# First 512 tokens loaded as four transposes of 512 by 256 and contracted in depth pairs, with the weight loads moved to another queue

## Chip, cores and metric

One core of one Trainium2 chip. The metric is device microseconds of one execution. All comparisons are between runs of the fast state, each with runs of the kernel before on the same chip. A ratio is the mean time of one kernel's fast runs over the mean of the other's in the same rounds, so it is not quite the ratio of the medians quoted beside it.

## The reference

Two attention blocks share one input x (2048 tokens, width 1024, bf16), and a gate mixes them.

```python
x = A_x
g = _sigmoid((x * gate_w).sum(-1, keepdims=True))
a = _A_ref(x, A_wqkv, A_wo)      # linear attention: qkv, phi, state, output projection
b = _B_ref(x, B_wqkv, B_wo)      # dilated local attention: qkv, 8 keys a query, output projection
return g * a + (1 - g) * b
```

What matters here is the first product of the kernel: v of block B, that is x @ B_wqkv[:, 2048:3072], 16 tiles of 128 tokens by two halves of 512 columns, each eight matmuls deep: 256 matmuls. It needs x transposed, depth on the partitions.

## The kernel before

The kernel records operations, and a list scheduler puts them in an order for each engine. `after` and the tiles that an operation reads and writes become waits on semaphores; `prio` orders operations that are ready.

```python
def load_x(t, prio):           # one tile of 128 tokens, all 1024 of depth: 256 KB, transposed by the DMA
    e_, r = t // 8, t % 8
    return P.op("sp", lambda e: e.dma_start_transpose(xT[:, :, t * 128:(t + 1) * 128], x2[e_, r * 128:(r + 1) * 128, :]), ...)

def load_w(slot, half, src, c0, prio, d0=0, d1=8, eng="sp", after=()):   # depth blocks d0 to d1: 128 KB each
    ...
load_x(0, 0)
load_w(0, 0, Bw, 2048, 0.1, 0, 2, "act")      # first weight half, four pieces: two from ScalarE
load_w(0, 0, Bw, 2048, 0.2, 2, 4, "act")
load_w(0, 0, Bw, 2048, 0.3, 4, 6)             # and two from Sync
load_w(0, 0, Bw, 2048, 0.4, 6, 8)
for t in range(1, NT):
    load_x(t, 3 + t)
for d in range(0, 8, 2):
    load_w(0, 1, Bw, 2560, 6.1 + 0.1 * d, d, d + 2)   # second weight half, Sync
# ... (cut)
for i in range(WARM):          # 9 matmuls on zeros, to raise the clock
    ...
for t, half in [(4 * b + i, half) for b in range(NT // 4) for half in range(2) for i in range(4)]:
    bank = main.next()
    step = 2 if t == 0 else 8
    for d in range(0, 8, step):
        o = group(bank, xs, w, [xr, ws[0].part((d, d + step), (half * 512, half * 512 + 512))], d, d + step)
    move(vt[:, :], bank.ap, 512, bank, vt.all())     # evict to SBUF, then store to HBM
```

In the profile, line 1313 is the matmul inside `group`, 1292 the DMA inside `load_w`, 1287 the transposing DMA of `load_x`.

Of the kernel before, what the change touches and what calls it, by code (L numbers as in the profile page):

```python
# [13 lines left out]
D = 1024  # L14
# [1088 lines left out]
def build_kernel(nc, A_x, A_wqkv, A_wo, B_x, B_wqkv, B_wo, gate_w, out):  # L1103
    del B_x
    S = A_x.shape[1]
    NT = S // 128
    HS = S // 2
    x2 = A_x[0].rearrange("(m e) d -> e m d", e=2)
# [5 lines left out]
    def SB(shape, dtype, name, at=None):  # L1114
        n = SZ[dtype]
        for d in shape[1:]:
            n *= d
        if at is None:
            at = base[0]
            base[0] += (n + 31) // 32 * 32  # L1120
        uid[0] += 1
        h = nc.alloc_sbuf_tensor_at("%s_%d" % (name, uid[0]), list(shape), dtype, offset=at)
        return Tile("S", h, at, list(shape), dtype)
# [34 lines left out]
    def hb(p0, p1, half):  # L1158
        return [("H%d" % half, p0, p1, None)]

    xT = SB([128, 8, S], BF16, "xT")
    qT = SB([128, 8, S], BF16, "qT")
    kT = SB([128, 8, S], BF16, "kT")
    ws = [SB([128, 8, 1024], BF16, "w%d" % i) for i in range(4)]
# [7 lines left out]
    gwb = SB([128, 1024], BF16, "gwb")  # L1172
# [30 lines left out]
    xn = Ring([SB([128, 1024], BF16, "xn%d" % i, at=az.t[i].lo) for i in range(2)])  # L1203
# [14 lines left out]
    act = lambda n: 0.19 + n / 1200.0  # L1218
    dps = lambda n: 0.14 + n / 960.0

    def plan(seen):

        P = Prog(nc, nc.alloc_semaphore)
# [58 lines left out]
        Bw = B_wqkv.rearrange("(dc p) f -> p dc f", p=128)  # L1282
        Bo = B_wo.rearrange("(dc p) f -> p dc f", p=128)

        def load_x(t, prio):
            e_, r = t // 8, t % 8
            return P.op("sp", lambda e: e.dma_start_transpose(xT[:, :, t * 128:(t + 1) * 128], x2[e_, r * 128:(r + 1) * 128, :]),  # L1287
                        1.5, writes=[xT.part((0, 8), (t * 128, (t + 1) * 128))], prio=prio, chan="x%d" % t, lat=1.3)

        def load_w(slot, half, src, c0, prio, d0=0, d1=8, eng="sp", after=()):  # L1290
            n = d1 - d0
            return P.op(eng, lambda e: e.dma_start(ws[slot][:, d0:d1, half * 512:half * 512 + 512], src[:, d0:d1, c0:c0 + 512]), 0.4 + 0.2 * n,  # L1292
                        writes=[ws[slot].part((d0, d1), (half * 512, half * 512 + 512))], prio=prio, chan="w%d_%d_%d" % (slot, half, d0), lat=0.55 * n, after=after)

        load_x(0, 0)
        load_w(0, 0, Bw, 2048, 0.1, 0, 2, "act")
        load_w(0, 0, Bw, 2048, 0.2, 2, 4, "act")
        load_w(0, 0, Bw, 2048, 0.3, 4, 6)
        load_w(0, 0, Bw, 2048, 0.4, 6, 8)
        for t in range(1, NT):  # L1300
            load_x(t, 3 + t)
        for d in range(0, 8, 2):
            load_w(0, 1, Bw, 2560, 6.1 + 0.1 * d, d, d + 2)
        P.op("sp", lambda e: e.dma_start(gwb[:, :], gate_w[None, :].to_broadcast([128, D])), 0.6, writes=[gwb.all()], prio=29, chan="gw", lat=0.8)


        main = Pool(banks[0:7])

        def group(bank, lhs, rhs, reads, lo=0, hi=8):
            def fn(e):  # L1310
                last = None
                for dc in range(lo, hi):
                    last = e.matmul(bank.ap(), lhs(dc), rhs(dc), start=(dc == 0), stop=(dc == 7))  # L1313
                return last
            return P.op("pe", fn, (hi - lo) * mm(512), reads=reads, writes=[bank.iv])
# [13 lines left out]
        def x_tile(t):  # L1329
            return (lambda dc: xT[:, dc, t * 128:(t + 1) * 128]), xT.part((0, 8), (t * 128, (t + 1) * 128))  # L1330

        def x_chunk(u):
            return (lambda dc: xT[:, dc, u * 512:(u + 1) * 512]), xT.part((0, 8), (u * 512, (u + 1) * 512))

        def w_half(slot, half):
            return (lambda dc: ws[slot][:, dc, half * 512:half * 512 + 512]), ws[slot].part((0, 8), (half * 512, half * 512 + 512))

        def w_cols(slot, j):
            return (lambda dc: ws[slot][:, dc, j * 128:(j + 1) * 128]), ws[slot].part((0, 8), (j * 128, (j + 1) * 128))
# [11 lines left out]
        for i in range(WARM):  # L1351
            P.op("pe", lambda e: e.matmul(banks[7].ap(), warm[:, 0:128], warm[:, :], start=True, stop=True), 0.43, reads=[warm.all()], writes=[banks[7].iv], prio=-1)


        early = {(2, 0): (1, 0, Bw, 1024, 21), (4, 1): (2, 0, Bw, 0, 22), (7, 1): (1, 1, Bw, 1536, 23), (10, 1): (2, 1, Bw, 512, 24),
                 (12, 1): (3, 0, Aw, 1024, 25), (14, 1): (3, 1, Aw, 1536, 26)}
        for t, half in [(4 * b + i, half) for b in range(NT // 4) for half in range(2) for i in range(4)]:
            vt, vs = vst.next()
            xs, xr = x_tile(t)
            bank = main.next()  # L1360
            w, wr = w_half(0, half)
            step = 2 if t == 0 else 8
            for d in range(0, 8, step):
                o = group(bank, xs, w, [xr, ws[0].part((d, d + step), (half * 512, half * 512 + 512))], d, d + step)
            move(vt[:, :], bank.ap, 512, bank, vt.all())
            P.op("sp", lambda e, t=t, vt=vt, half=half: e.dma_start(vB_hbm[t * 128:(t + 1) * 128, half * 512:half * 512 + 512], vt[:, :]), 0.6, reads=[vt.all()],
                 writes=[hb(t * 128, (t + 1) * 128, half)], chan="vst%d" % vs, lat=0.5, prio=5)
            if (t, half) in early:
                load_w(*early[t, half], after=[o])
        load_w(0, 0, Aw, 2048, 30)  # L1370
        load_w(0, 1, Aw, 2560, 31)


        for t in range(NT):
            xt, xs_ = xn.next()
            P.op("sp", lambda e, t=t, xt=xt: e.dma_start(xt[:, :], x2[t // 8, (t % 8) * 128:(t % 8) * 128 + 128, :]), 0.6, writes=[xt.all()], chan="xn%d" % xs_, lat=1.0)
            P.op("dve", lambda e, t=t, xt=xt: e.scalar_tensor_tensor(out=xt[:, :], in0=xt[:, :], scalar=1.0, in1=gwb[:, :], op0=ALU.mult, op1=ALU.mult,
                                                                      accum_out=gt[:, t:t + 1]), dps(1024), reads=[xt.all(), gwb.all()], writes=[xt.all(), gt.part((t, t + 1))],
                 prio=1000 + len(P.ops) + 80)
# [7 lines left out]
        main = Pool(banks[0:4])  # L1387
# [80 lines left out]
        for e_ in range(2):  # L1468
            if True:
                for j in range(8):  # L1470
                    for isq in range(2):
                        for u in (2 * e_, 2 * e_ + 1):
                            bank = main.next()
                            w, wr = w_cols(1 + isq, j)
                            xs, xr = x_chunk(u)
# [10 lines left out]
        for c in range(4):  # L1486
            for I in range(2):
                P.op("sp", lambda e, c=c, I=I: e.dma_start(ws[1][32 * c:32 * c + 32, 4 * I:4 * I + 4, :],
                                                           A_wo[512 * I + 128 * c:512 * I + 128 * c + 128, :].rearrange("(r e) f -> e r f", e=32)), 0.6,
                     writes=[ws[1].part((4 * I, 4 * I + 4), (0, 1024))], prio=40, chan="wo%d_%d" % (c, I), lat=0.9)  # L1490
# [25 lines left out]
        for t in range(NT):  # L1516
            pkt, _ = pk.next()
            azt, _ = az.next()
            xs, xr = x_tile(t)
            for r in range(4):  # L1520
                bank = main.next()
                w, wr = w_half((3, 0)[r // 2], r % 2)
# [16 lines left out]
        main = Pool(banks)  # L1539
# [158 lines left out]
    for _ in range(PASSES):  # L1698
        got = plan(seen)
        seen = got[2]  # L1700
        if best is None or got[0].span < best[0].span:
            best = got
    P, flag_op = best[:2]
# [52 lines left out]
```

## Time and profile before

| | before |
|---|---|
| median of 6 runs | 495.50 us (495.07 to 496.56) |
| span of the profiled run | 493.6 us |
| first real matmul | 5.62 us |
| second tile of x landed | 7.97 us |
| second weight half landed | 14.70 us |
| first matmul of the k projection (end of the first product) | 61.80 us |
| from there to the end | 431.83 us |

The last three rows matter most. The first product is 256 matmuls, 0.2158 us from start to start when nothing holds them: 55.24 us. From 5.62 to 61.80 it took 56.18, so 0.94 us were lost there. The landing times come from the records of the DMA semaphores in the trace; the lines of the profile are shown in the prediction.

### The profile page before, as it was taken

To read this page: it belongs to the slowest core of one execution; us is meant where nothing else is said; L and a number is where in the kernel's file an instruction comes from. 1 tells how busy PE (TensorE), PEld (TensorE's weight loads), DVE (VectorE), ACT (ScalarE), POOL (GpSimd) and SP (SyncE) were. 2 spreads that over 40 slices of the span, in tenths; PEclk is the share of its full clock that TensorE was granted. 3 is DMA by queue.
4 is the path that set the end of the run, shared out by engine and by line. 5 is a ranking of instruction groups with operands and counts; after the bars stand their busy time and mean duration, and the time that the engine had idled before them with its cause. 6 is when DMAs were issued, how large, how long until landed. Compare 5 with 4: busy or idle time off the path is not lost.

```text
span 493.6 us, 11394 instructions
## 1 busy us (share of the span) xinstructions
PE 477.7 (97%) x5055; PEld 226.2 (46%) x5121; DVE 274.7 (56%) x487; ACT 166.9 (34%) x287; POOL 5.1 (1%) x27
## 2 busy tenths in 40 slices
PE   8999999999999999999999999999999999999995
PEld 3444444444444445545554544444444444444442
DVE  2112345899676785564555555596865735524443
ACT  2111111222334345656565465455432223020000
POOL 3000000000000000000000000000000000000000
PEclk9999999999999999999999999999999999999999
DMA  8989992222003155111010100503564325101122
GB/s 225 212 206 322 307 371 62 86 86 85 14 23 110 29 161 141 28 36 35 24 35 25 35 3 3 171 1 80 124 182 117 76 38 153 65 1 66 65 85 68
DMA packets 51067, 48.80 MB, mean 99 GB/s; under 512 B 20161, under 2 KB 38977, under 8 KB 51010
## 3 DMA queue, kind: packets, MB, share of 16 engines
q1 hardware_dynamic: 50466, 47.47, 34.5%
q8 instruction: 42, 0.69, 0.6%
q10 hardware_dynamic: 544, 0.52, 0.3%
q14 instruction: 15, 0.12, 0.1%
HBM read 34.34 MB, written 9.44 MB: 89 GB/s over the span
## 4 chain that ended last, share of the span: by engine, by line
PE 89%; DMA 3%; SPq 3%; issue 2%; DVE 2%; ACT 1%; ACTq 0%
PE ps_all L1313 71%; PE ps_all L1634 11%; PE ps_all L1405 2%; PE ps_all L1424 2%; DMA rb<-rc_hbm 1%; SPq L1287 1%; PE ps_all L1506 1%; SPq L1598 1%; DMA w<-in_B_wqkv_dram 1%; PE ps_all L1431 1%; DMA rc_hbm<-ra 1%; DVE zsel L1548 1%; SPq L1292 1%; DVE pq L1326 0%; PE ps_all L1585 0%
## 5 line engine op out<-in xcount | busy, mean ns | idle before, releaser
L1313 PE MATMUL ps_all<-w,xT 128*128 128x512 bf16 x921 | 207.5, 380 | 5.4 <-issue 4.3
L1313 PE MATMUL ps_all<-xT,w 128*128 128x512 bf16 x748 | 167.5, 379 | 2.3 <-issue 1.7
L1313 PEld LDWEIGHTS ps_all<-w,xT 128*128 128x128 bf16 x960 | 91.3, 98 | 109.8 <-DMA xT<-in_A_x_dram 1.8
L1313 PEld LDWEIGHTS ps_all<-xT,w 128*128 128x128 bf16 x768 | 73.7, 98 | 89.1 <-issue 1.8
L1634 PE MATMUL ps_all<-w,qT 128*128 128x512 bf16 (+1 forms) x259 | 55.3, 373 | 0.3
L1634 PEld LDWEIGHTS ps_all<-w,qT 128*128 128x128 bf16 x264 | 25.8, 98 | 29.7
L1324 DVE TENSOR_SCALAR e<-e 128x512 bf16<-128x512 bf16 x64 | 18.3, 291 | 33.8 <-ACT e L1320 17.2
L1344 DVE CAST vst<-ps_all 128x512 bf16<-128x512 f32 x15 | 10.4, 692 | 44.0 <-PE ps_all L1313 44.0
L1411 ACT ACTIVATE E<-ps_all 128x1824 bf16<-128x1824 f32 (+1 forms) x18 | 30.4, 1687 | 9.8 <-PE ps_all L1405 9.0
L1322 ACT ACTIVATE e<-ps_all 128x512 bf16<-128x512 f32 x32 | 19.1, 597 | 42.8 <-PE ps_all L1313 42.8
L1414 DVE TENSOR_TENSOR E<-E,msk 128x1824 bf16<-128x1824 bf16 (+1 forms) x18 | 19.8, 1102 | 22.1 <-ACT E L1411 22.1
L1638 DVE SCALAR_TENSOR_TENSOR o<-ps_all,gm,xT 128x512 bf16<-128x512 f32 (+1 forms) x25 | 18.2, 730 | 23.0 <-PE ps_all L1634 22.8
L1320 ACT ACTIVATE e<-ps_all 128x512 bf16<-128x512 f32 x32 | 19.1, 597 | 26.8 <-PE ps_all L1313 25.8
L1345 ACT ACTIVATE vst<-ps_all 128x512 bf16<-128x512 f32 x17 | 10.1, 597 | 47.7 <-PE ps_all L1313 47.7
L1274 DVE TENSOR_TENSOR mx<-mx,kT 128x1024 bf16<-128x1024 bf16 x32 | 20.8, 688 | 9.3 <-ACT kT L1345 9.2
L1274 DVE TENSOR_TENSOR mx<-mx,qT 128x1024 bf16<-128x1024 bf16 x32 | 20.8, 687 | 6.9 <-ACT qT L1348 6.7
L1443 DVE TENSOR_TENSOR qT<-ps_all,L 128x456 bf16<-128x456 f32 (+1 forms) x36 | 21.0, 627 | 6.2 <-ACT L L1441 5.0
L1326 DVE SCALAR_TENSOR_TENSOR pk<-ps_all,e 128x512 bf16<-128x512 f32 x32 | 21.9, 688 | 0.7
L1440 ACT ACTIVATE L<-ps_all 128x456 f32<-128x456 f32 (+1 forms) x36 | 17.8, 547 | 12.4 <-PE ps_all L1424 12.4
L1345 ACT ACTIVATE kT<-ps_all 128x512 bf16<-128x512 f32 x16 | 9.6, 597 | 35.8 <-PE ps_all L1313 35.8
L1601 DVE TENSOR_TENSOR xT<-xT,rb 128x512 bf16<-128x512 bf16 x24 | 16.3, 689 | 8.7 <-DMA rb<-rc_hbm 8.5
L1348 ACT ACTIVATE qT<-ps_all 128x512 bf16<-128x512 f32 x16 | 9.6, 597 | 31.5 <-PE ps_all L1313 31.5
(72 smaller groups left out, 284.1 us busy)
## 6 DMA issues: line engine op xcount, KB each, us to landing
rb<-rc_hbm SPq DMA_DIRECT2D x32, 256.0 KB, 5.1
w<-in_A_wqkv_dram SPq DMA_DIRECT2D x6, 1024.0 KB, 8.5
v<-vB_hbm SPq DMA_DIRECT2D x36, 128.0 KB, 2.9
vB_hbm<-vst SPq DMA_DIRECT2D x32, 128.0 KB, 5.9
w<-in_B_wqkv_dram SPq DMA_DIRECT2D x4, 1024.0 KB, 9.0
xn<-in_A_x_dram SPq DMA_DIRECT2D x16, 256.0 KB, 2.7
out_dram<-o SPq DMA_DIRECT2D x15, 256.0 KB, 2.0
w<-in_A_wo_dram SPq DMA_DIRECT2D x8, 256.0 KB, 4.1
```

Of the source, the lines that this page charges most:

```text
L1274: P.op("dve", lambda e, m=m, op=op: e.tensor_tensor(m[:, 0:n], m[:, 0:n], src, op), 0.08 + n / 1920.0, reads=[m.all(), reg], writes=[m.all()],
L1313: last = e.matmul(bank.ap(), lhs(dc), rhs(dc), start=(dc == 0), stop=(dc == 7))
L1320: P.op("act", lambda e: e.activation(e_[:, :], bank.ap(), ACT.Exp), act(512), reads=[bank.iv], writes=[e_.all()])
L1322: P.op("act", lambda e: e.activation(e_[:, :], bank.ap(), ACT.Exp, accum_out=qe[:, col:col + 1]), act(512) + 0.1, reads=[bank.iv], writes= ...
L1324: P.op("dve", lambda e: e.tensor_scalar(e_[:, :], e_[:, :], 1.0, 1e-6, op0=ALU.min, op1=ALU.add), 0.25, reads=[e_.all()], writes=[e_.all()])
L1326: P.op("dve", lambda e: e.scalar_tensor_tensor(out=dst, in0=bank.ap(), scalar=0.0, in1=e_[:, :], op0=ALU.max, op1=ALU.add), dps(512), read ...
L1345: fa = lambda e: e.activation(dst, src(), ACT.Copy)
L1411: P.op("act", lambda e: e.activation(E[:, 0:32 * nq].rearrange("p (j q) -> p j q", j=4), ps[:, 4:8, 0:8 * nq], ACT.Exp), act(32 * nq), rea ...
L1414: P.op("dve", lambda e: e.tensor_tensor(ev(), ev(), m[:, :, :].rearrange("p r q -> p (r q)")[:, None, :].to_broadcast([128, 16, 2 * nq]), ...
L1443: P.op("dve", lambda e, L=L, h=h, q0=q0: e.tensor_tensor(qT[:, :, q0:q0 + nq], SO[h].ap(0, n).rearrange("p (c q) -> p c q", c=8), L[:, 0:n ...
L1634: last = e.matmul(bank.ap(0, f1 - f0), qT[:, dc, t * 128:(t + 1) * 128], ws[3][:, dc, f0:f1], start=(dc == 0), stop=(dc == 7))
L1638: P.op("dve", lambda e, bank=bank, o_=o_, t=t, n=n, i0=i0, i1=i1, tgt=tgt, c0=c0: e.scalar_tensor_tensor(out=o_[:, i0 * 128:i1 * 128].rear ...
```

## The change

Its intent is to have the start consume the loads as they come: four transposing loads of 512 tokens by 256 of depth, so that after the first of them four banks can each take two matmuls; a block of eight tiles, so that the second weight half is wanted later; and later loads held back so that they don't compete. All four first weight pieces and the second weight half now come from ScalarE's queue. Cut to its core:

```diff
-        load_x(0, 0)
-        load_w(0, 0, Bw, 2048, 0.1, 0, 2, "act")
-        load_w(0, 0, Bw, 2048, 0.2, 2, 4, "act")
-        load_w(0, 0, Bw, 2048, 0.3, 4, 6)
-        load_w(0, 0, Bw, 2048, 0.4, 6, 8)
-        for t in range(1, NT):
-            load_x(t, 3 + t)
         for d in range(0, 8, 2):
-            load_w(0, 1, Bw, 2560, 6.1 + 0.1 * d, d, d + 2)
+            load_w(0, 0, Bw, 2048, 0.1 + 0.1 * d, d, d + 2, "act")
+            P.op("sp", lambda e, d=d: e.dma_start_transpose(xT[:, d:d + 2, 0:512], x2[0, 0:512, 128 * d:128 * d + 256]), ...)
+        for t in range(4, 8):
+            load_x(t, 4 + t)
 ...
-        for t, half in [(4 * b + i, half) for b in range(NT // 4) for half in range(2) for i in range(4)]:
+        for t, half in [(t, half) for t0, n in ((0, 8), (8, 4), (12, 4)) for half in range(2) for t in range(t0, t0 + n)]:
+            if t < 4 and half == 0:
+                if t == 0:
+                    first = [main.next() for _ in range(4)]
+                    for d in range(0, 8, 2):
+                        for t_ in range(4):
+                            if d == 6 and t_ == 0:
+                                o_w = o
+                            o = group(first[t_], x_tile(t_)[0], w, [...], d, d + 2)
+                    for d in range(0, 8, 4):
+                        load_w(0, 1, Bw, 2560, 3 + 0.1 * d, d, d + 4, "act", after=[o_w])
+                bank = first[t]
 ...
+                if (t, half) == (5, 0):
+                    for t_ in range(8, NT):
+                        load_x(t_, 4 + t_, [o])
```

(Cut: assumed DMA durations of the scheduler; the loads of gate_w and of plain x, which also wait for tile 5; and the load of the next weight slot, now tied to the second half of tile 1 and not to the first of tile 2.) In the changed kernel `group` is line 1309 and the new transposes are line 1297.

More of the change, by code (lines that the diff above doesn't have):

```diff
@@ L1283, in plan, with load_x @@
         Bo = B_wo.rearrange("(dc p) f -> p dc f", p=128)
-        def load_x(t, prio):
+        def load_x(t, prio, after=()):
             e_, r = t // 8, t % 8
             return P.op("sp", lambda e: e.dma_start_transpose(xT[:, :, t * 128:(t + 1) * 128], x2[e_, r * 128:(r + 1) * 128, :]),
-                        1.5, writes=[xT.part((0, 8), (t * 128, (t + 1) * 128))], prio=prio, chan="x%d" % t, lat=1.3)
+                        1.5, writes=[xT.part((0, 8), (t * 128, (t + 1) * 128))], prio=prio, chan="x%d" % t, lat=1.15, after=after)
         def load_w(slot, half, src, c0, prio, d0=0, d1=8, eng="sp", after=()):
@@ L1292, in load_w @@
             return P.op(eng, lambda e: e.dma_start(ws[slot][:, d0:d1, half * 512:half * 512 + 512], src[:, d0:d1, c0:c0 + 512]), 0.4 + 0.2 * n,
-                        writes=[ws[slot].part((d0, d1), (half * 512, half * 512 + 512))], prio=prio, chan="w%d_%d_%d" % (slot, half, d0), lat=0.55 * n, after=after)
-        load_x(0, 0)
-        load_w(0, 0, Bw, 2048, 0.1, 0, 2, "act")
-        load_w(0, 0, Bw, 2048, 0.2, 2, 4, "act")
-        load_w(0, 0, Bw, 2048, 0.3, 4, 6)
-        load_w(0, 0, Bw, 2048, 0.4, 6, 8)
-        for t in range(1, NT):
-            load_x(t, 3 + t)
-        for d in range(0, 8, 2):
-            load_w(0, 1, Bw, 2560, 6.1 + 0.1 * d, d, d + 2)
-        P.op("sp", lambda e: e.dma_start(gwb[:, :], gate_w[None, :].to_broadcast([128, D])), 0.6, writes=[gwb.all()], prio=29, chan="gw", lat=0.8)
+                        writes=[ws[slot].part((d0, d1), (half * 512, half * 512 + 512))], prio=prio, chan="w%d_%d_%d" % (slot, half, d0), lat=0.42 * n, after=after)
+        for d in range(0, 8, 2):
+            load_w(0, 0, Bw, 2048, 0.1 + 0.1 * d, d, d + 2, "act")
+            P.op("sp", lambda e, d=d: e.dma_start_transpose(xT[:, d:d + 2, 0:512], x2[0, 0:512, 128 * d:128 * d + 256]),
+                 1.3, writes=[xT.part((d, d + 2), (0, 512))], prio=d / 2, chan="xd%d" % d, lat=1.2)
+        for t in range(4, 8):
+            load_x(t, 4 + t)
         main = Pool(banks[0:7])
@@ L1352, in plan @@
             P.op("pe", lambda e: e.matmul(banks[7].ap(), warm[:, 0:128], warm[:, :], start=True, stop=True), 0.43, reads=[warm.all()], writes=[banks[7].iv], prio=-1)
-        early = {(2, 0): (1, 0, Bw, 1024, 21), (4, 1): (2, 0, Bw, 0, 22), (7, 1): (1, 1, Bw, 1536, 23), (10, 1): (2, 1, Bw, 512, 24),
+        early = {(1, 1): (1, 0, Bw, 1024, 21), (4, 1): (2, 0, Bw, 0, 22), (7, 1): (1, 1, Bw, 1536, 23), (10, 1): (2, 1, Bw, 512, 24),
                  (12, 1): (3, 0, Aw, 1024, 25), (14, 1): (3, 1, Aw, 1536, 26)}
-        for t, half in [(4 * b + i, half) for b in range(NT // 4) for half in range(2) for i in range(4)]:
+        for t, half in [(t, half) for t0, n in ((0, 8), (8, 4), (12, 4)) for half in range(2) for t in range(t0, t0 + n)]:
             vt, vs = vst.next()
             xs, xr = x_tile(t)
-            bank = main.next()
             w, wr = w_half(0, half)
-            step = 2 if t == 0 else 8
-            for d in range(0, 8, step):
-                o = group(bank, xs, w, [xr, ws[0].part((d, d + step), (half * 512, half * 512 + 512))], d, d + step)
+            if t < 4 and half == 0:
[5 more added lines that the diff above has]
+                                o_w = o
+                            o = group(first[t_], x_tile(t_)[0], w, [xT.part((d, d + 2), (t_ * 128, t_ * 128 + 128)), ws[0].part((d, d + 2), (0, 512))], d, d + 2)
+                    for d in range(0, 8, 4):
+                        load_w(0, 1, Bw, 2560, 3 + 0.1 * d, d, d + 4, "act", after=[o_w])
+                bank = first[t]
+            else:
+                bank = main.next()
+                o = group(bank, xs, w, [xr, ws[0].part((0, 8), (half * 512, half * 512 + 512))])
+                if (t, half) == (5, 0):
+                    x_op = o
+                    for t_ in range(8, NT):
+                        load_x(t_, 4 + t_, [o])
             move(vt[:, :], bank.ap, 512, bank, vt.all())
@@ L1369, in plan @@
                 load_w(*early[t, half], after=[o])
+        P.op("sp", lambda e: e.dma_start(gwb[:, :], gate_w[None, :].to_broadcast([128, D])), 0.6, writes=[gwb.all()], prio=29, chan="gw", lat=0.8, after=[x_op])
         load_w(0, 0, Aw, 2048, 30)
@@ L1375, in plan @@
             xt, xs_ = xn.next()
-            P.op("sp", lambda e, t=t, xt=xt: e.dma_start(xt[:, :], x2[t // 8, (t % 8) * 128:(t % 8) * 128 + 128, :]), 0.6, writes=[xt.all()], chan="xn%d" % xs_, lat=1.0)
+            P.op("sp", lambda e, t=t, xt=xt: e.dma_start(xt[:, :], x2[t // 8, (t % 8) * 128:(t % 8) * 128 + 128, :]), 0.6, writes=[xt.all()], chan="xn%d" % xs_, lat=1.0, after=[x_op])
             P.op("dve", lambda e, t=t, xt=xt: e.scalar_tensor_tensor(out=xt[:, :], in0=xt[:, :], scalar=1.0, in1=gwb[:, :], op0=ALU.mult, op1=ALU.mult,
```

## The prediction

> **What bounds the kernel now.** I read the page first: the shares of busy time, then the chain that ended last.
>
> ```profile
> PE 477.7 (97%) x5055; PEld 226.2 (46%) x5121; DVE 274.7 (56%) x487; ACT 166.9 (34%) x287; POOL 5.1 (1%) x27
> ...
> PE 89%; DMA 3%; SPq 3%; issue 2%; DVE 2%; ACT 1%; ACTq 0%
> ```
>
> TensorE is busy 97% of a 493.6 us span and carries 89% of the chain. A change to the loads can win only time in which TensorE waits or runs slowly, and this change touches only the start. So next I read the chain in order of time for the first 60 us.
>
> ```profile
> 4.64 2.18 SPq L1287
> ...
> 9.36 0.47 SPq L1292
> ...
> 9.87 4.83 DMA w<-in_B_wqkv_dram
> 14.70 0.05 issue
> 14.74 0.61 PE ps_all L1313 x2
> 15.35 0.05 issue
> 15.40 10.74 PE ps_all L1313 x49
> ```
>
> Up to 14.7 us the chain runs through load issues on the Sync queue and then a weight load; after that it is matmuls in unbroken pieces. This looks like 14 us of load-bound start, but it is not: a chain says what released the last wait, not how long the wait was. So I read how the weight loads of TensorE stand in time from 5 to 18 us.
>
> ```profile
> 5.62 0.13 PEld L1313 LDWEIGHTS ps_all<-w,xT 128*128 128x128 bf16 x2 [1.26 <-DMA xT<-in_A_x_dram]
> 6.02 0.15 PEld L1313 LDWEIGHTS ps_all<-w,xT 128*128 128x128 bf16 x1 [0.28 <-issue]
> 6.45 0.15 PEld L1313 LDWEIGHTS ps_all<-w,xT 128*128 128x128 bf16 x1 [0.28 <-issue]
> 6.76 0.75 PEld L1313 LDWEIGHTS ps_all<-w,xT 128*128 128x128 bf16 x4 [0.15 <-issue]
> 8.02 5.72 PEld L1313 LDWEIGHTS ps_all<-w,xT 128*128 128x128 bf16 x28 [0.51 <-DMA xT<-in_A_x_dram]
> 14.00 0.17 PEld L1313 LDWEIGHTS ps_all<-w,xT 128*128 128x128 bf16 x2 [0.26 <-DMA w<-in_B_wqkv_dram]
> 14.74 3.35 PEld L1313 LDWEIGHTS ps_all<-w,xT 128*128 128x128 bf16 x17 [0.56 <-DMA w<-in_B_wqkv_dram]
> ```
>
> The real work starts at 5.62 us. Two waits follow, for the second x tile (until 8.02) and for the second weight half (until 14.74). The bracketed gaps overstate them, because weight loads run ahead of the matmuls. I therefore measured start to start of the matmul records. Steady spacing is 0.216 us (28 of them from 8.02 run at that). Above it stand: 5.621 to 6.753 us, three intervals of which two are at about 0.43, an excess of 0.48 us; 7.618 to 8.019, an excess of 0.185; 14.288 to 14.741, an excess of 0.237. Sum 0.90 us. The first evictions of the banks check this:
>
> ```profile
> 8.04 0.60 ACT L1345 ACTIVATE vst<-ps_all 128x512 bf16<-128x512 f32 x1 [4.99 <-PE ps_all L1313]
> ...
> 9.96 0.60 ACT L1345 ACTIVATE vst<-ps_all 128x512 bf16<-128x512 f32 x1 [1.32 <-PE ps_all L1313]
> ...
> 11.68 0.69 DVE L1344 CAST vst<-ps_all 128x512 bf16<-128x512 f32 x1 [5.78 <-PE ps_all L1313]
> ...
> 13.41 0.60 ACT L1345 ACTIVATE vst<-ps_all 128x512 bf16<-128x512 f32 x1 [2.86 <-PE ps_all L1313]
> ...
> 15.38 0.60 ACT L1345 ACTIVATE vst<-ps_all 128x512 bf16<-128x512 f32 x1 [1.38 <-PE ps_all L1313]
> ```
>
> A group of eight matmuls takes 1.73 us when nothing holds it (11.68 to 13.41). Group two came 1.92 after group one and group five 1.97 after group four: excesses of 0.19 and 0.24, the same two waits. So the whole start holds 0.90 us to be won behind the first matmul, 0.18% of the span, and of these 0.48 are not a wait.
>
> **What the Trainium skill says.** First, "TensorE: Matmul & The Clock Gate", section "What's actually happening": the array runs at half clock until it has been busy for about one free-running window of 3413 ns. The trace agrees: warm-up matmuls from 1.25 us at 0.427 spacing, full clock recorded from 6.62 us. That is the 0.48 us: the first three intervals of real work straddle the switch. Second, the same page, "Wait — 56ns, not 53.3ns?", gives 215.7 ns start to start for 512 warm columns; the trace has 216. Third, "DMA: Bandwidth & Descriptors", section "Issuing engines are not separate DMA queues": loads issued from ScalarE and Sync share the same 16 engines, so moving a load to another issuer saves issue time alone. The trace agrees: while the second weight piece (ScalarE) and the first transpose (Sync) were both in flight, each half microsecond moved about 110 packets of 1 KB and 144 of 256 B, against some 560 small ones for a transpose alone. Fourth, same page, "Latency and other measured facts": a transposing load was measured there at 261 GB/s. This trace has 1024 packets of 256 B, 18 ns each on 16 engines: 1.15 us for 256 KB, or 228 GB/s; I use that.
>
> **The change, part by part.**
>
> *Start of the first matmul.* Before, it needs tile 0 transposed (256 KB) and the first weight piece (256 KB). After, it needs the first transpose of 512 by 256 (256 KB) and the same weight piece. Before, these land at 5.58 and 3.53 us. In the new one the transpose is again the first on Sync at 0.8 us, beside the same two first ScalarE loads. If it also makes 1024 packets of 256 B, as its size suggests, it lands at about 5.6. No gain and no loss: 0.0 us. This is my least certain term, since no transposing load of this shape is in the trace.
>
> *Clock.* Warm-up and start stay, so about 0.48 us of half speed stays: 0.0.
>
> *Second wait.* Before, matmul 9 needs tile 1, landed at 7.97; by then the engines had moved four weight pieces and two transposes. After, matmul 9 needs the second transpose; the four weight pieces now come all from ScalarE beside it, so when it lands the engines have moved at most the same six transfers. Four pieces at 256 x 48 ns / 16 = 0.77 us and two transposes at 1.15 are 5.4 us of engine time in both kernels. So it lands at 7.9 to 8.1 and the 0.185 us wait mostly stays; if the transposes get more of the engines, up to 0.18 is won. I take -0.05.
>
> *Later depth pairs.* Third and fourth transpose land at about 9.1 and 10.3 (1.15 apart); needed at 8.02 + 1.73 = 9.75 and 11.5. No wait. The pieces are eight matmuls long, against two in before, so each covers its successor's load.
>
> *Second weight half.* Before, it is 1 MB in four pieces behind three tiles, wanted after 32 matmuls: the 0.237 us wait. After, a block of eight tiles puts it behind 64 matmuls, at about 5.6 + 64 x 0.216 + 0.7 = 20.1 us. It is issued when the third depth pair is done, about 11.5, and its engine time is 3.1 us. This wait goes: -0.24.
>
> *Tiles 4 to 7.* They follow at 1.15 us on the queue, so the fourth ends near 14.9 if alone; needed at 13.4, 15.1, 16.8, 18.5. The second weight half is in flight with tiles 6 and 7. Two transposes and 1 MB of weights are 5.4 us of engine time from about 12.1, ending near 17.5 plus 0.4 of landing: 18.0 against the 18.5 at which tile 7 is wanted. It fits, by half a microsecond. 0.0.
>
> *Everything later.* The order of TensorE's matmul groups after the first stage is the same in both builds; the differences on VectorE and ScalarE are swapped copies up to the first attention block, where both have slack (56% and 34% busy). Later x tiles, now held until tile 5 is done, are wanted from 34 us on and issued from 17: no cost.
>
> Sum: -0.05 - 0.24 = -0.3 us. From the measured 495.43 that is **495.1 us**.
>
> **The rivals.**
>
> (1) The start is load-bound and the change removes all of it. For: the chain shows loads up to 14.7 us, and the wanted bytes per matmul fall, since each weight piece now serves four tiles. Against: TensorE was at its steady spacing for all but 0.42 us of waiting. At most 0.42 plus some of the clock's 0.48: 494.5 to 495.0.
>
> (2) The new shape lands later: short rows of 512 B, or four weight pieces ahead of the first transpose on the shared engines. For: the 30% share that a transpose got beside weights. Against: the second piece was as much beside it before. If it lands 1 us later, TensorE also idles longer before its clock rises: 496 to 497.
>
> (3) The freed waits return as one for tile 6 or 7 beside the second weight half (margin 0.5 us by my sum): 495.3 to 496.
>
> (4) The clock switches elsewhere in its free-running window: half a microsecond either way, in either kernel; with the before runs spread from 495.07 to 496.56 this alone hides the gain.
>
> **Range and chances.** Centre 495.1. Half a microsecond of spread for clock and runs, half for the landing of the new transpose, added as independent about 0.7; for 8 in 10 that is 494.2 to 496.1. Two per cent is 9.9 us, over ten times what the start holds; only a failure of the new loads could be that slow. Faster 0.005, same 0.985, slower 0.01.
>
> **What would show it.** In the new profile: first real matmul at 5.4 to 5.9 us with a wait for xT; a remaining wait for xT before the ninth matmul of at most 0.3; no wait for w near matmul 65; no wait for tiles 4 to 7; steady 1.73 us per group from about 8 us on; first k projection about 0.3 us earlier than 61.80. I would be wrong if the first transpose lands after 6.5, if full clock comes later than 7.5, or if a wait appears at tiles 6 or 7.

## The result, and the profile after

The changed kernel took 499.90 us (median of 6 runs, 498.04 to 501.45) against 495.50 (6 runs, 495.07 to 496.56): ratio 1.0086, 95% interval 1.006 to 1.0112. It is slower by 4.4 us, less than 2% but clear of the noise, and outside the predicted range.

From the page of the changed kernel, the shares of busy time and the chain that ended last:

```profile
PE 480.8 (96%) x5055; PEld 227.4 (46%) x5121; DVE 276.7 (55%) x489; ACT 165.8 (33%) x285; POOL 5.1 (1%) x27
...
PE 88%; DMA 4%; SPq 3%; DVE 2%; issue 2%; ACT 0%; ACTq 0%
```

Nothing stands out: one per cent less TensorE, one more DMA. The chain in order of time (start, length, what) of the changed kernel says where:

```profile
13.21 9.29 DMA xT<-in_A_x_dram
22.50 0.14 issue
22.63 9.19 PE ps_all L1309 x34
```

One transposing load, issued at 13.21 us, ended a wait at 22.50: more than nine microseconds, where the kernel before shows 3.8 as the median of its sixteen. It is tile 7. The weight loads of TensorE in the changed kernel (columns: start, length, engine and line, count, idle time before and what ended it):

```profile
6.22 0.14 PEld L1309 LDWEIGHTS ps_all<-w,xT 128*128 128x128 bf16 x2 [1.85 <-issue]
6.63 0.15 PEld L1309 LDWEIGHTS ps_all<-w,xT 128*128 128x128 bf16 x1 [0.27 <-issue]
...
10.35 9.60 PEld L1309 LDWEIGHTS ps_all<-w,xT 128*128 128x128 bf16 x45 [0.16 <-issue]
22.60 1.51 PEld L1309 LDWEIGHTS ps_all<-w,xT 128*128 128x128 bf16 x8 [2.65 <-issue]
24.38 0.15 PEld L1309 LDWEIGHTS ps_all<-w,xT 128*128 128x128 bf16 x1 [0.27 <-issue]
...
27.34 2.69 PEld L1309 LDWEIGHTS ps_all<-w,xT 128*128 128x128 bf16 x13 [0.24 <-issue]
```

Read the lines with x1: a load by itself every 0.43 us is a matmul at half clock. The start shows that until 10.35 us (in before until 6.75), and after the pause before 22.60 it comes again, until 27.34. The clock records agree: full from 10.23, half from 23.88 to 27.29.

The balance of this run against before: first matmul 0.63 us later (6.25 against 5.62); half clock 3.6 us against 0.5; the wait for tile 7, 2.35 us, against two small ones of 0.4 together. The k projection starts at 67.48 against 61.80, 5.68 later, and from there to the end it is 431.66 against 431.83. So the loss is in the first product, all of it.

What the DMA engines did shows in the stretches (columns: stretch, its length, busy time of the five engines, clock, mean DMA share, GB/s). Before:

```profile
5.00:7.00 2.00, 1.65 (x6) 0.56 (x6) 0.43 (x2) 0.00 (x0) 0.61 (x3) 1.00 1.15 308
7.00:9.00 2.00, 1.98 (x10) 0.77 (x9) 0.00 (x0) 0.60 (x1) 0.00 (x0) 1.00 1.12 250
...
15.00:20.00 5.00, 4.95 (x24) 2.29 (x24) 0.69 (x1) 1.19 (x2) 0.00 (x0) 1.00 0.87 208
```

And the changed kernel:

```profile
5.00:7.00 2.00, 1.02 (x3) 0.28 (x3) 0.43 (x2) 0.00 (x0) 0.63 (x3) 1.00 1.17 211
7.00:9.00 2.00, 2.00 (x6) 0.73 (x5) 0.00 (x0) 0.00 (x0) 0.00 (x0) 1.00 1.31 204
...
15.00:20.00 5.00, 4.95 (x24) 2.25 (x23) 1.59 (x3) 1.19 (x2) 0.00 (x0) 1.00 1.18 146
```

The last two columns are to be read together. The engines are busier (1.18 against 0.87 from 15 to 20 us) and move less (146 GB/s against 208). The records of the single packets say how: a 1 KB piece of weights took 46 to 48 ns when its kind was alone; from 15.5 to 17 us of the changed kernel the mean was 210 to 350 ns, and 50 to 97 ns for the 256 B pieces of the transposes, which take 18 alone. In both stretches (5 to 9 and 15 to 20 us) transposes from Sync and plain weight loads from ScalarE are in flight together. The second profile of the same kernel (changed_again, below) is milder in the later one: 50 to 108 ns for weights from 15.5 to 21 us, and 202 GB/s.

**Theory A**: transposing and plain loads on two queues at once share the 16 engines badly. The engines lose throughput, and the loads that are wanted later (third and fourth weight piece, second weight half) take the time of those wanted now (second transpose, tile 7). **Rivals**: the new shape of 512 by 256 is slow in itself; there are simply too many bytes; the size of the pieces; the idle gap ahead of the first matmul and the clock it costs.

### The profile page after: what moved, and what is told of

Read it like the earlier page. It is cut to its first block, busy times and chain, and to the rows that moved or that the text cites. A ratio compares the mean times of both kernels' runs of the same rounds, so it can differ in the third digit from the quotient of the medians.

```text
span 499.1 us, 11394 instructions
## 1 busy us (share of the span) xinstructions
PE 480.8 (96%) x5055; PEld 227.4 (46%) x5121; DVE 276.7 (55%) x489; ACT 165.8 (33%) x285; POOL 5.1 (1%) x27
## 4 chain that ended last, share of the span: by engine, by line
PE 88%; DMA 4%; SPq 3%; DVE 2%; issue 2%; ACT 0%; ACTq 0%
PE ps_all L1309 70%; PE ps_all L1645 11%; PE ps_all L1416 2%; PE ps_all L1435 2%; DMA xT<-in_A_x_dram 2%; SPq L1297 2%; DMA rb<-rc_hbm 1%; PE ps_all L1517 1%; SPq L1609 1%; SPq L1287 1%; DMA rc_hbm<-ra 1%; PE ps_all L1442 1%; DVE zsel L1559 1%; DVE pq L1322 0%; PE ps_all L1596 0%
## 5 line engine op out<-in xcount | busy, mean ns | idle before, releaser
L1309 PE MATMUL ps_all<-w,xT 128*128 128x512 bf16 x921 | 210.4, 384 | 8.1 <-issue 4.3
L1340 DVE CAST vst<-ps_all 128x512 bf16<-128x512 f32 x17 | 11.6, 691 | 48.5 <-PE ps_all L1309 48.5
L1422 ACT ACTIVATE E<-ps_all 128x1824 bf16<-128x1824 f32 (+1 forms) x18 | 30.4, 1688 | 10.2 <-PE ps_all L1416 9.5
L1341 ACT ACTIVATE vst<-ps_all 128x512 bf16<-128x512 f32 x15 | 9.0, 597 | 53.3 <-PE ps_all L1309 53.3
```

Source lines behind the costliest of these rows:

```text
L1309: last = e.matmul(bank.ap(), lhs(dc), rhs(dc), start=(dc == 0), stop=(dc == 7))
L1341: fa = lambda e: e.activation(dst, src(), ACT.Copy)
L1422: P.op("act", lambda e: e.activation(E[:, 0:32 * nq].rearrange("p (j q) -> p j q", j=4), ps[:, 4:8, 0:8 * nq], ACT.Exp), act(32 * nq), rea ...
```

## The experiments

Landing times (us) from the profiled run of each kernel; for the kernel before and its variant the second column is tile 1. "Lost" is the start of the k projection minus the first matmul minus 55.24; "waits" are the pauses in it, less one spacing each, and "half clock" what the matmul intervals in half-clock time exceed 0.216 us by. Each row is one profile, so a difference of some tenths between rows is not a finding.

| kernel | 2nd transpose | tile 7 | 2nd weight half | first matmul | lost | half clock | waits | rest to the end |
|---|---|---|---|---|---|---|---|---|
| before | 7.97 | not in this stage | 14.70 | 5.62 | 0.94 | 0.5 | 0.4 | 431.83 |
| changed | 9.40 | 22.49 | 23.79 | 6.25 | 5.99 | 3.6 | 2.35 | 431.66 |
| changed_again | 9.22 | 22.07 | 23.08 | 5.87 | 4.26 | 0 | 1.67 + 2.57 | 431.72 |
| w1_on_sync | 9.88 | 17.43 | 22.23 | 5.58 | 2.90 | 0 | 2.60 + 0.25 | 432.56 |
| w1_after_x7 | 9.76 | 16.86 | 22.61 | 5.54 | 3.33 | 0 | 2.54 + 0.76 | 431.81 |
| w1_quarters | 11.64 | 19.95 | 24.32 | 5.61 | 6.05 | 1.9 | 4.16 | 432.22 |
| warm12 | 10.26 | 22.52 | 22.99 | 5.99 | 4.58 | 0 | 2.58 + 1.98 | 431.85 |
| two_on_sync | 6.42 | 20.22 | 19.55 | 5.58 | 6.55 | 2.8 | 0.23 + 3.46 | 431.14 |
| both_on_sync | 6.47 | 16.77 | 20.95 | 5.49 | 1.72 | 0 | 0.59 + 1.08 | 431.74 |
| before_four_scalar | 9.97 | not in this stage | 15.75 | 6.12 | 4.28 | 2.9 | 1.40 | 432.29 |
| sync_ordered | 6.32 | 15.85 | 20.69 | 5.62 | 0.78 | 0.8 | none | 431.44 |
| ordered_warm6 | 6.39 | 15.95 | 21.42 | 5.66 | 1.32 | 1.3 | none | 430.87 |

The last column moves by up to 1.7 us from run to run without order, in kernels whose later part is the same in TensorE's order. It is noise to the times, and the reason to read the "lost" column beside them.

### changed_again: the changed kernel once more

> The changed kernel once more, for a second profile of it: in the first the clock stayed at half speed until 10.2 us and hid the wait for the second transpose. If that was chance: full clock near 5 to 7 us and an open wait of 2 to 3 us after the first eight matmuls, and again a wait for tile 6 or 7 of 2 us or more; 498 to 501 us. If the half clock is the rule for this kernel: full clock at 9 to 11 us again and no open wait there.

498.91 us (one run). The matmuls of the first product (start, length, line, count, idle before):

```profile
5.87 1.89 PE L1309 MATMUL ps_all<-w,xT 128*128 128x512 bf16 x8 [1.06 <-DMA xT<-in_A_x_dram]
9.27 10.53 PE L1309 MATMUL ps_all<-w,xT 128*128 128x512 bf16 x48 [1.51 <-DMA xT<-in_A_x_dram]
22.21 41.17 PE L1309 MATMUL ps_all<-w,xT 128*128 128x512 bf16 x190 [2.40 <-DMA xT<-in_A_x_dram]
```

Here the clock was full from 4.2 us, and the wait for the second transpose lies open: eight matmuls, a pause of 1.5 us (1.67 from start to start, a little under the 2 to 3 expected), 48 matmuls, a pause of 2.4 for tile 7. In the first profile the half clock had covered the first pause. So the long half clock at the start does not belong to this kernel (the last point of this document says what decided it), and the two late transposes do.

### w1_on_sync: second weight half from Sync

```diff
-load_w(0, 1, Bw, 2560, 3 + 0.1 * d, d, d + 4, "act", after=[o_w])
+load_w(0, 1, Bw, 2560, 3 + 0.1 * d, d, d + 4, after=[o_w])
```

> The changed kernel with the second weight half issued from the Sync queue, behind the eight transposes, instead of from ScalarE beside them. Theory A (plain loads of one queue and transposes of the other slow each other down when they share the engines): tile 7 lands near 16.5 us instead of 22.5, the weight half near 20, the wait of 2.35 us before tile 7's matmuls and the second half-clock window (1.68 us) go: about 496 us. Theory B (there are simply too many bytes at that moment): tile 7 is early but the weight half then lands at 23 to 24 us and TensorE waits for it as long: 499 to 500 us.

497.58 us (497.0 to 498.56, 4 runs) against 495.22: ratio 1.0045 (1.0026 to 1.0063).

```profile
5.58 1.90 PE L1309 MATMUL ps_all<-w,xT 128*128 128x512 bf16 x8 [0.31 <-DMA xT<-in_A_x_dram]
9.93 53.31 PE L1309 MATMUL ps_all<-w,xT 128*128 128x512 bf16 x245 [2.44 <-DMA xT<-in_A_x_dram]
```

Tile 7 landed at 17.43, and after 9.93 only 0.25 us of waiting is left, for the weight half: the pause for tile 7 is gone, as theory A said. The time fell by less than expected, since the pause for the second transpose stays in this kernel. Because that pause shifts the matmuls, the weight half at 22.23 was just in time; the run alone does not decide against too many bytes.

### w1_after_x7: second weight half from ScalarE, but only when tile 7 has landed

```diff
-load_w(0, 1, Bw, 2560, 3 + 0.1 * d, d, d + 4, "act", after=[o_w])
+load_w(0, 1, Bw, 2560, 3 + 0.1 * d, d, d + 4, "act", after=[x7_op])
```

> The changed kernel with the second weight half still from ScalarE, but issued only when tile 7 has landed. Theory A: tile 7 lands near 16.5 us, the two weight pieces, alone on the engines but for the stores, within 5 us of it, about 21 us; a wait of under 1 us remains: 496 to 497 us. Theory A' (the ScalarE queue's loads of this size are slow in themselves): the pieces take 8 to 10 us as in the changed kernel and TensorE waits until 25 us: above 501 us.

498.14 us (497.65 to 498.71, 4 runs): ratio 1.006 (1.0043 to 1.0077).

```profile
9.80 12.26 PE L1309 MATMUL ps_all<-w,xT 128*128 128x512 bf16 x56 [2.38 <-DMA xT<-in_A_x_dram]
22.66 40.53 PE L1309 MATMUL ps_all<-w,xT 128*128 128x512 bf16 x187 [0.60 <-DMA w<-in_B_wqkv_dram]
```

The same queue, the same pieces, apart in time only: tile 7 landed at 16.86, and the weight half 5.7 us after its issue at 16.89, where it took 10.2 in both profiles of the changed kernel. So ScalarE's queue is not slow in itself; being in flight together is what costs. The time is above what was expected, by the pause for the second transpose that I had not counted into either of these two expectations.

### w1_quarters: second weight half in four pieces

```diff
-for d in range(0, 8, 4):
-    load_w(0, 1, Bw, 2560, 3 + 0.1 * d, d, d + 4, "act", after=[o_w])
+for d in range(0, 8, 2):
+    load_w(0, 1, Bw, 2560, 3 + 0.1 * d, d, d + 2, "act", after=[o_w])
```

> The changed kernel with the second weight half cut into four pieces of 256 KB instead of two of 512 KB, still from ScalarE beside tiles 6 and 7. If the piece size made the slow packets: tile 7 lands before 19 us and the time falls to about 496. If it is the two queues together (theory A): tile 7 still lands after 20 us, 499 to 501 us.

499.70 us (498.5 to 500.9, 4 runs): ratio 1.008 (1.0061 to 1.0098). No gain in time. But in its profiled run the second transpose came only at 11.64, so that the pieces were issued at 17.0 us, late enough to leave tile 7 alone for the most part. The profile therefore does not say what the piece size does: inconclusive.

### warm12: twelve warm-up matmuls

```diff
-WARM = 9
+WARM = 12
```

> The changed kernel with twelve warm-up matmuls instead of nine, so that TensorE works on until about 6.4 us and no idle gap comes before the first real matmul. If the gap kept the clock at half speed for one more window: full clock at 6.4 to 7.2 us instead of 10.2, about 1.4 us faster than the changed kernel: 498.0 to 498.8 us. Rival (the clock rises late for another reason): full clock again at about 10 us and no gain, 499.5 to 500.5 us.

499.86 us (499.12 to 501.88, 4 runs): ratio 1.0103 (1.0076 to 1.013). A miss. The clock was full from 5.63 us and no half clock was lost, and yet no time was won, because the wait for the second transpose (2.58 us) then lay open, as in changed_again. The losses do not add: slow matmuls during a wait for data cost nothing more. The clock is not the cause of the 4.4 us.

### two_on_sync: third and fourth weight piece from Sync

```diff
-load_w(0, 0, Bw, 2048, 0.1 + 0.1 * d, d, d + 2, "act")
+load_w(0, 0, Bw, 2048, (0.1, 0.3, 1.5, 2.5)[d // 2], d, d + 2, "act" if d < 4 else "sp")
```

> The changed kernel with the third and fourth weight piece issued from the Sync queue between the transposes (first, second transpose, piece, third transpose, piece, fourth), so that after 5 us one queue alone carries the start; the second weight half still comes from ScalarE beside tiles 6 and 7. Theory A (transposes beside another queue's plain loads are slow): the second transpose lands at 6.7 to 7.5 us instead of 9.4 to 11.6, no wait after the first eight matmuls, 2.4 us won; the wait before tile 7 of about 2 us stays or grows, since TensorE comes there earlier: 497 to 498.5 us. Rival (the new 512 by 256 shape is slow in itself): the second transpose still lands after 9 us and nothing is won, 499 to 500 us.

501.06 us (500.24 to 501.4, 4 runs) against 495.09: ratio 1.0114 (1.0094 to 1.0134).

```profile
5.58 10.76 PE L1309 MATMUL ps_all<-w,xT 128*128 128x512 bf16 x47 [0.42 <-DMA xT<-in_A_x_dram]
19.64 43.58 PE L1309 MATMUL ps_all<-w,xT 128*128 128x512 bf16 x185 [3.29 <-DMA xT<-in_A_x_dram]
```

The step was right and the time wrong. The second transpose landed at 6.42, one microsecond after the first: the shape of 512 by 256 is not slow, that rival falls, and the start runs with one pause of 0.23 us. But TensorE was then ahead; the second weight half, tied to the 24th matmul, was issued at 10.95 instead of 13.57, and fell on tile 6 as well as on tile 7. Tile 6 landed at 19.59, TensorE stood for 3.46 us, and the clock stayed at half for two windows (18.57 to 25.39), another 2.8. Mending the first fault alone made the second one worse.

### both_on_sync: both of them

The two edits above together (w1_on_sync and two_on_sync).

> Both loads put on the Sync queue: third and fourth weight piece between the transposes, and the second weight half behind tile 7. Theory A: no wait of over half a microsecond is left in the first stage, and the time is that of the prediction for the change, 494.6 to 495.6 us, within 0.1% of the kernel before. Rival (the shape, the depth pairs or the block of eight cost by themselves): over 496.5 us.

495.95 us (495.38 to 498.99, 6 runs) against 495.09: ratio 1.0027 (1.0001 to 1.0054).

```profile
11.27 8.81 PE L1309 MATMUL ps_all<-w,xT 128*128 128x512 bf16 x39 [0.43 <-DMA xT<-in_A_x_dram]
21.00 41.61 PE L1309 MATMUL ps_all<-w,xT 128*128 128x512 bf16 x188 [0.92 <-DMA w<-in_B_wqkv_dram]
```

Most of the loss is gone with the shape, the depth pairs and the block of eight all in place. But it misses what theory A expected: two waits of over half a microsecond are left (0.6 and 1.1 us), and the time lies between the two ranges; by the ratio it is still slower than the kernel before. One of the waits shows a finer grain: the fourth weight piece, sent behind the third transpose in the same queue, landed 1.58 us after it, though it has 0.77 us of packets.

### before_four_scalar: one part of the change alone

```diff
-load_w(0, 0, Bw, 2048, 0.3, 4, 6)
-load_w(0, 0, Bw, 2048, 0.4, 6, 8)
+load_w(0, 0, Bw, 2048, 0.3, 4, 6, "act")
+load_w(0, 0, Bw, 2048, 0.4, 6, 8, "act")
```

> The kernel before, its tiles, order and blocks untouched, with one thing of the change: third and fourth weight piece come from ScalarE instead of Sync. Theory A: the old-shaped transposes beside them are slowed as well; the second tile lands at 9 us or later instead of 7.97, TensorE waits 1 us or more for it: 496 to 498 us. Rival (the new shape is the cause): second tile at 8 us or earlier, since two plain loads no longer stand ahead of it in its queue, and 494.5 to 495.5 us.

497.20 us (496.43 to 499.67, 4 runs) against 495.09: ratio 1.0029 (1.0008 to 1.005). The ratio leaves out the profiled run, which was the slowest of the four.

```profile
6.13 2.72 PE L1313 MATMUL ps_all<-w,xT 128*128 128x512 bf16 x6 [0.86 <-DMA xT<-in_A_x_dram]
9.83 53.39 PE L1313 MATMUL ps_all<-w,xT 128*128 128x512 bf16 x233 [0.98 <-DMA w<-in_B_wqkv_dram]
```

Its stretches (last column GB/s; the kernel before moved 308 and 250):

```profile
5.00:7.00 2.00, 1.14 (x4) 0.35 (x4) 0.43 (x2) 0.00 (x0) 0.63 (x3) 1.00 1.10 231
7.00:9.00 2.00, 1.84 (x5) 0.33 (x3) 0.00 (x0) 0.00 (x0) 0.00 (x0) 1.00 1.23 205
```

With the old tiles and the old order, moving two plain loads of 256 KB to the other queue brings the second tile from 7.97 to 9.97 us, though in its own queue two loads fewer stand ahead of it. It was the last of the same six loads in both kernels, so here the order explains nothing: the six took 2.0 us longer. The time is in the expected range, but the wait is not the expected one. The pause of 1.40 us was for the fourth weight piece (the second line of the matmuls; it landed at 9.78, against 7.18 before), and the tile was wanted only at 10.66. The rest of the loss is half clock until 13.6 us, 2.9 us of it; how much of that the other three runs had (496.43 to 497.63 us) is not known.

### plain_in_place: plain loads instead of the four transposes

A wrong result on purpose (relative error 0.72), one run with a profile (494.89 us, state unknown).

```diff
-e.dma_start_transpose(xT[:, d:d + 2, 0:512], x2[0, 0:512, 128 * d:128 * d + 256])
+e.dma_start(xT[:, d:d + 2, 0:512], x2[0, 64 * d:64 * d + 128, :].rearrange("p (a b) -> p a b", a=2))
```

> Wrong results on purpose: the changed kernel with its four 512 by 256 transposes replaced by plain loads of the same 256 KB each (untransposed), everything else as in the changed kernel, the four weight pieces from ScalarE. If any two queues at once slow each other down: the second x load lands at 8.5 us or later, as in the changed kernel (9.4). If it takes a transpose beside plain loads: it lands at 6 to 7.5 us and the six transfers are done at 320 GB/s or so.

The second x load landed at 6.24 us. The stretches (last column GB/s):

```profile
5.00:7.00 2.00, 2.00 (x7) 0.73 (x7) 0.43 (x2) 0.00 (x0) 0.62 (x3) 1.00 1.09 376
```

The same two queues, the same issuers and bytes, and 376 GB/s against 211. (Transposes alone moved 287 from 7 to 8 us of the kernel before, so part of this gap is theirs anyway; one queue with both kinds moved 308 from 5 to 7 us of it.) Packets of both queues took 46 to 51 ns from 4.5 to 8 us. So two queues at once are not slow in themselves. Two things besides the transposing differ here, the size of the pieces, which the next run takes up, and the time to issue a load, 0.5 us against 1.3, which none separates.

### small_plain2: plain loads in pieces of 256 B

A first kernel for this did not build (its access pattern had too many dimensions). The second writes beside the x tile, which is set to zero: a wrong result on purpose, one run.

```diff
-e.dma_start_transpose(xT[:, d:d + 2, 0:512], x2[0, 0:512, 128 * d:128 * d + 256])
+e.dma_start(qT[:, d, 0:1024].rearrange("p (b c) -> p b c", c=128), xw[64 * d:64 * d + 128, :, 0, :])
```

> Wrong results on purpose, and a second try at a kernel that did not build: the changed kernel with plain loads in place of its four transposes, now each of 1024 pieces of 256 B, the transposes' own packet size, written beside the x tile (which is set to zero); everything else as in the changed kernel. If it is the transposing that does not mix with plain loads: packets stay near 18 and 48 ns and the second x load lands at 7 to 8 us. If it is small packets beside large ones from another queue: both kinds take far longer while both queues are active and the second x load lands at 9 us or later, as in the changed kernel.

```profile
5.00:7.00 2.00, 1.49 (x7) 0.61 (x7) 0.49 (x2) 0.00 (x0) 1.79 (x10) 1.00 1.17 290
7.00:9.00 2.00, 1.37 (x8) 0.44 (x6) 0.43 (x2) 0.00 (x0) 0.51 (x3) 1.00 1.26 260
```

Between the two: the second x load landed at 8.26 us (6.24 with plain loads, 9.22 and 9.40 in the changed kernel), small packets kept 18 to 20 ns, and 1 KB packets took 55 to 65 from 5 to 8 us. The changed kernel moved 211 and 204 GB/s in these stretches. So the packet size takes a part and the transposing another. Which is larger is not shown: by the landing it is the size, by the packet times the transposing (1 KB packets took up to 130 ns in the changed kernel then), and by what moved from 5 to 9 us they are about equal (351 GB/s with plain loads, 275 here, 207 and 214 in the changed kernel). Its time of 499.75 us comes mostly from the other collision: tile 7, a real transpose, and the second weight half from ScalarE; tile 7 landed at 21.20.

### sync_ordered: fewer switches between kinds

```diff
-(0.1, 0.3, 1.5, 2.5)[d // 2]
+(0.1, 0.3, 1.5, 1.6)[d // 2]
 ...
-o = group(bank, xs, w, [xr, ws[0].part((0, 8), (half * 512, half * 512 + 512))])
+step = 4 if (t, half) == (0, 1) else 8
+for d in range(0, 8, step):
+    o = group(bank, xs, w, [xr, ws[0].part((d, d + step), (half * 512, half * 512 + 512))], d, d + step)
```

That is both_on_sync with the queue of Sync reordered: two transposes, two weight pieces, six transposes, the second weight half.

> The version with both loads on the Sync queue, with the switches between plain loads and transposes cut down: first and second transpose, then third and fourth weight piece together, then the other six transposes, then the second weight half; and the first group of the second half starts on the first of its two pieces. In the version before it TensorE still waited 0.9 us for that weight half and 0.6 us for transposes. If these go, the first stage holds only the clock's share: 494.3 to 495.3 us, at or just under the kernel before. If the second weight half still lands after 20.8 us: 495.3 to 496.2.

494.84 us (494.24 to 496.58, 6 runs) against 495.46 (11 runs): ratio 0.9993 (0.9976 to 1.0011).

```profile
5.62 56.19 PE L1309 MATMUL ps_all<-w,xT 128*128 128x512 bf16 x251 [0.35 <-DMA xT<-in_A_x_dram]
```

One line for the whole first product: no wait in it, 0.78 us lost, all of it clock. This is what the change was meant to do. Against before it is 0.16 us less lost, and the interval holds 1: not shown to be faster.

### ordered_warm6: six warm-up matmuls

```diff
-WARM = 9
+WARM = 6
```

> The previous version with six warm-up matmuls instead of nine, so that TensorE is idle for about 1.7 us ahead of the first real matmul and nothing else changes. If an idle gap before the start costs one more window at half clock: full clock near 8 to 10 us instead of 5 to 6.6, and 1 to 1.7 us slower than with nine. If the clock depends on something else: the same time within 0.5 us.

494.39 us (493.58 to 496.37, 4 runs): ratio to before 0.9982 (0.9957 to 1.0008). A miss: not slower than with nine. The profile shows full clock at 8.33 us against 7.21 and 0.5 us more lost; the rest of the kernel was 0.6 us shorter, within the scatter of that column. What a gap ahead of the start costs depends on where it falls in time, and the last point of this document puts numbers to that.

## Why the prediction was wrong

**The frame was right.** Only the first product moved; the rest is 431.66 us against 431.83. No more than 0.9 us could be won there, and a version without the fault lands where the prediction put the change (494.84 against 495.1), although its gain over before is within the noise.

**Start of the first matmul: right.** I called the new shape the least certain term. It landed at 5.4 to 6.1 us in all kernels that have it, and where no plain load was in flight beside it the second one followed 0.8 to 1.0 us later. Rival (2) came near: it named the weight pieces on the shared engines, but looked for the delay at the first transpose.

**Second wait: this step failed.** It said that the second transpose lands at 7.9 to 8.1, because the engines have moved at most the same six transfers and "5.4 us of engine time in both kernels". Engine time was added up as if a packet cost the same beside any other, on any queue. (Its 1.15 us for a transpose is a misreading of its own. At its 560 packets in half a microsecond, 1024 take 0.91 us; 560 of 18 ns are 0.63 us for each of 16 engines, so packets overlap and their times cannot simply be added. That made the sum too long and hid part of the fault. Its 30% share of a transpose beside weights is 25% of the bytes.) The same six transfers took until 9.2 to 11.6 us in the six profiles with the changed kernel's start, and until 9.97 in the kernel before with its two loads moved. What moved from 5 to 9 us says the same: 254 to 282 GB/s in the five profiles with both kinds in one queue (before among them), 148 to 218 in the seven with weight pieces from ScalarE beside the transposes. When one queue puts the second transpose ahead of two of the pieces, it lands at 6.3 to 6.5. The term of -0.05 us was a wait of 1.7 to 4.2 us in the five profiles in which the full clock left it open.

**Tiles 4 to 7: the same sum failed, and the order.** "It fits, by half a microsecond" used the same sum, 18.0 us for tile 7; it landed at 22.1 to 22.5 in the three profiles of the changed kernel's own timing (changed, changed_again, warm12). The sum went wrong in its start, 12.1, since tile 5 had landed only at 14.8 to 15.5, and in its length: tiles 6 and 7 and the weight half took 7.4 to 9.0 us from there and not 5.9. But they took 6.9 to 7.8 us with all of it on Sync too. What the second queue changed most was the order: tile 7 landed 2.1 to 2.8 us after tile 5 when the weights stood behind it, and 6.6 to 7.7 when they came beside it. The rival (3) named the right collision and sized it at 0.2 to 0.9 us over the prediction. It was 2.0 to 2.6 us of waiting, and up to 1.7 us of half clock after it (23.70 to 27.33 us held nine intervals of which each should take 0.216). So two of the prediction's own signs of being wrong came: full clock later than 7.5 us, and a wait at tile 7.

**Second weight half: -0.24, won and meaningless.** The wait for w did go. Putting it later in TensorE's order moved the load onto the transposes of tiles 6 and 7.

**What the trace had offered.** Two signs were there. In the kernel before, where its queue goes from transposes to the second weight half (9.5 to 10 us), 24 packets of weights took 233 ns each. And the third citation of the prediction took "the same 16 engines" as a licence to add; it looked at 3.5 to 5 us, where the two kinds do run together at their usual packet times (in the changed kernel 53 to 56 and 18 to 23 ns), and carried that to all later times.

**What is shown and what is argued.** Shown: the two loads from ScalarE cause the loss (both_on_sync takes most of it away and sync_ordered the rest, before_four_scalar makes it in the old kernel), being in flight together is what matters (w1_after_x7), and plain loads on both sides do not make it (plain_in_place; small_plain2 in part). The Trainium skill, "DMA: Bandwidth & Descriptors", section "Queues, rings and completion order", says that each engine goes round its queues packet by packet; that would make an engine switch kinds all the time where one queue switches once, and a switch that costs would explain both the packet times and the 1.58 us of both_on_sync. That is argued: no record here tells which engine a packet ran on, and why the first 1.5 us of overlap are free is open. So two things stand side by side: at the start the engines moved less, and at tile 7 it was for the most part plain sharing. In two_on_sync, too, tiles 6, 7 and the weight half had landed 6.9 us after tile 5, in both_on_sync 7.0; nothing was lost in sum, but the tile wanted first came last.

## What to carry to other kernels

A queue is also an order: loads in one queue came here in the order of need, while a second issuer lets the later-wanted load share with the one that TensorE stands at, so move a load to another queue only where it may share. In this kernel it also paid to keep plain loads away from transposing ones in flight, on another queue most of all, and to put like with like inside one queue. Where a prediction adds engine times of unlike transfers, look first for a place in the trace where the two kinds meet, and read share and GB/s together there: busier engines that move less are the sign.

## What the Trainium skill lacked or had wrong

- "DMA: Bandwidth & Descriptors", section "Issuing engines are not separate DMA queues": it says that a second issuer saves only issue time. It also changes who waits: with two loads of 256 KB moved from Sync to ScalarE and nothing else changed, the second tile landed at 9.97 us instead of 7.97.
- The same page, "Rules for kernel authors": "A transpose next to ordinary DMAs needs nothing" speaks of right results, and these were right (in every kernel here but the two made wrong on purpose). It does not hold for the time: from 5 to 9 us 148 to 218 GB/s moved with transposes in one queue and plain loads in the other, 254 to 282 with both in one queue. No page has this cost.
- No page gives the cost of going from transposes to plain loads in one queue: the weight piece behind a transpose landed 0.9 to 1.6 us after it (six cases in the four kernels with pieces on Sync), against 0.77 us of packets.
- "TensorE: Matmul & The Clock Gate", "What's actually happening": the page has the clock fall after an idle window, but a pause shorter than a window can cost one. Its free-running window fits these traces: half-clock stretches in mid-run were 3.41 or 6.83 us long. So I laid windows of 3.41 us back and forth from the recorded changes of the clock, in all fourteen profiles, and added up the time without a matmul in each (the records' ends are modelled, so to a tenth or so). At half clock, all 18 windows with at most 0.74 us of it were followed by full clock, and the six with 0.86 to 1.07 were not. At full clock, windows with up to 1.89 us kept it, and those with 2.16 and more lost it. So the pause for tile 7 in the changed kernel, with 2.16 us in one window, cost 1.7 us of half clock. The longer one in changed_again, cut into 1.47 and 0.93 by the end of a window, cost none. Where the window ends is luck: the 0.98 us gap ahead of the start fell in one window in the changed kernel, and in changed_again the clock was full before the gap came.
